# The output projection over two chunks of tokens at a time, with seven block products in place of eight

## The chip, the cores and the metric

The kernel runs on one NeuronCore of one Trainium2 chip. The metric is the device time of one execution in microseconds; 256 and 512 below are columns of a tile, and a tile has up to 128 partitions.

## The reference, cut to what matters

```python
xn = _layernorm(x)                                   # S = 2048 tokens, D = 640
q, k, v = split(xn @ wqkv)                           # H = 32 heads of 20
phi_q = concat(softmax(q @ w_phi), softmax(-(q @ w_phi)))
phi_k = concat(softmax(k @ w_phi), softmax(-(k @ w_phi)))
kv, z = sum_s phi_k * v, sum_s phi_k
o = (phi_q @ kv) / (phi_q @ z + 1e-6)
s = o @ wo                                           # the output projection
g = silu(gelu(xn @ w1 + b1) @ w2 + b2)
return x + s * g
```

The change concerns `s = o @ wo` and what feeds it.

## The kernel before

Everything is computed transposed: features in partitions, tokens in columns. The 2048 tokens are four chunks of 512, worked in the order 2, 3, 0, 1 (`ORDER`). A product in full precision is made of three matmuls (`PASSES`): each operand is split into a high part, rounded by ScalarE (ACT) with a copy, and a low part, what is left, made by a subtraction on VectorE (DVE) or GpSimd (POOL).

The kernel first makes keys, values and queries, then runs twelve units of the gated MLP (six slices of the hidden features, for each half of the tokens), and at last the output projection. From the MLP on, every engine's order is that of the code (`manual_schedule`): each engine works its queue in the order written, and an instruction waits for semaphores of the instructions that it depends on. SP issues all the DMAs of this stretch, so a DMA that waits for its data holds all DMAs behind it.

The attention's numerators belong to the projection's stretch. The normalised query features of a chunk lie in DRAM (`phi_t`); `load_phi` brings them in six tiles `phT`, `num` multiplies each by the state (`bdk`, `bdl`) into a bank of PSUM, ACT copies the high part (`oT[:, 0]`), DVE subtracts to get the low part (`oT[:, 1]`). Five tiles j of 128 rows and a last one of 120 (`oTl`, which holds the remaining 40 rows in three forms) make one chunk. `finish(c, d, oT, last)` is one output tile: chunk c, column block d of five, 16 matmuls into one bank (three for each of five row blocks of `wo`, one for the last rows), a multiplication by the gate on DVE, an addition of the residual on POOL, and the output's DMA. The second half of the tokens (chunks 2 and 3, worked first) reads its gates from DRAM (`gt`); for chunks 0 and 1 ACT makes them in place (`y`). `load_res` loads residual and gate four outputs ahead. Features for a later chunk are loaded in the middle of the chunk before the one that precedes it, and the numerators of the next chunk are computed after its fourth output. The last token tile's features are normalised (`late_q`, `q_norm`) while the first chunk is projected: POOL multiplies, DVE reduces and inverts, POOL scales, DVE transposes, and SP writes them to DRAM.

The pools: `slabs` and `late` hold tiles of 128 x 1024, `rows` is a ring of eleven tiles of up to 704 columns (residuals, gates, raw weights), and eight banks of PSUM rotate (`bankB`). A tile that takes a slot waits for whatever still uses that slot, an output's DMA for instance.

## Time and profile before

| what | value |
|---|---|
| runs, us | 650.24, 650.43, 650.50 (median 650.43) |
| profiled execution, span from first to last instruction | 649.0 us, so that 1.4 us of the median lie around it |
| mean granted TensorE clock | 0.999 |
| TensorE (PE) busy | 643.7 us, 99% |
| DVE, ACT, POOL busy | 485.1 (75%), 238.1 (37%), 408.9 (63%) us |
| DMA, mean over the span | 210 GB/s |
| the last matmuls of the MLP end, the projection's begin | at about 555 us |

A busy share is an average over the span; the stages differ. In the rows below a line such as L1156 is the line of the kernel that recorded the instruction, "pB<-oT,wo" names what is written and read, and PEld is TensorE's loading of weights, which overlaps its matmuls. The matrix products of the numerators are in plain float32 and stand as two records for each instruction. SPq is the queue of SP, from which the DMAs are issued.

### The profile page before, as it was taken

Reading aid. Unit: us, or ns where it says so; the run is one execution under the profiler, and the core shown is the slowest. Engines: PE = TensorE matmul, PEld = TensorE weight load, DVE = VectorE, ACT = ScalarE, POOL = GpSimd, SP = SyncE. Lnnn points to the kernel's source line nnn. Section 1 sums busy time; section 2 is a strip of 40 time slices with the busy share of each in tenths; the row PEclk is TensorE's granted clock in tenths of the full one; section 3 lists DMA queues with packets and bytes.
Section 4 is the critical chain, followed back from the end, with each engine's and each line's share of the span. In section 5 each row is a group of like instructions: output and inputs, shape, how many; then the busy total and the mean of one; then the engine's idle time right before and its main releaser. Section 6 shows DMA issues by size and latency. Waiting matters only on the chain.

```text
span 649.0 us, 11412 instructions
## 1 busy us (share of the span) xinstructions
PE 643.7 (99%) x4379; PEld 559.1 (86%) x4379; DVE 485.1 (75%) x736; ACT 238.1 (37%) x345; POOL 408.9 (63%) x375
## 2 busy tenths in 40 slices
PE   9999999999999999999999999999999999999997
PEld 9999999999999998888888888888888886766866
DVE  5887976789867787587988877768889899853132
ACT  3622423425243447244243346641231524032130
POOL 2876477897987756857878865355463966342321
PEclk9999999999999999999999999999999999999999
DMA  9477286494312477365986998794969499999952
GB/s 346 113 238 228 57 303 197 107 309 147 123 42 74 152 263 262 103 217 170 317 236 236 254 409 285 144 350 163 183 238 243 67 267 198 304 242 248 291 207 81
DMA packets 167119, 136.53 MB, mean 210 GB/s; under 512 B 89890, under 2 KB 131106, under 8 KB 166682
## 3 DMA queue, kind: packets, MB, share of 16 engines
q1 hardware_dynamic: 164330, 124.22, 65.9%
q10 hardware_dynamic: 2736, 11.60, 4.8%
q8 instruction: 34, 0.56, 0.4%
q14 instruction: 19, 0.16, 0.1%
HBM read 87.41 MB, written 48.38 MB: 209 GB/s over the span
## 4 chain that ended last, share of the span: by engine, by line
PE 96%; DMA 1%; DVE 1%; SPq 0%; issue 0%; DVEq 0%
PE pB L998 24%; PE pA L411 23%; PE pB L969 23%; PE pB L1156 11%; PE pA L724 6%; PE pB L1103 2%; PE pA L174 2%; PE kv L491 2%; PE qV L724 1%; DMA folds<-in_wqk_dram 1%; PE qY L724 1%; DVE y L1007 1%; PE pB L1110 1%; DMA phi_t<-eq 0%; PE pA L397 0%; DVE wolh L1080 0%
## 5 line engine op out<-in xcount | busy, mean ns | idle before, releaser
L998 PE MATMUL pB<-hs,w2s 128*128 128x512 f32 x720 | 165.7, 389 | 0.0
L998 PEld LDWEIGHTS pB<-hs,w2s 128*128 128x128 f32 x720 | 135.0, 188 | 28.8 <-DVE y L1007 0.8
L969 PE MATMUL pB<-xp,w1s 128*128 128x512 f32 x324 | 81.3, 389 | 0.0
L969 PE MATMUL pB<-xd,w1s 128*128 128x512 f32 x324 | 79.3, 389 | 0.0
L452 POOL TENSOR_TENSOR eq<-eq,rc 128x1280 f32<-128x1280 f32 x16 | 37.9, 2368 | 55.3 <-DVE rc L1060 38.1
L1156 PE MATMUL pB<-oT,wo 128*128 128x512 f32 (+1 forms) x315 | 72.3, 381 | 0.0
L969 PEld LDWEIGHTS pB<-xd,w1s 128*128 128x128 f32 x324 | 60.8, 188 | 12.6
L969 PEld LDWEIGHTS pB<-xp,w1s 128*128 128x128 f32 x324 | 60.8, 188 | 12.6
L1156 PEld LDWEIGHTS pB<-oT,wo 128*128 128x128 f32 x315 | 57.2, 188 | 13.8 <-PE pB L1103 2.5
L1007 DVE TENSOR_TENSOR y<-pB,y 128x512 f32<-128x512 f32 x100 | 63.1, 676 | 1.4 <-PE pB L998 1.4
L974 ACT ACTIVATE pB<-pB,b1t 128x512 f32<-128x512 f32 x48 | 31.8, 662 | 78.8 <-DVE pB L1237 28.9
L411 PE MATMUL pA<-wk,xp 128*128 128x320 f32 x384 | 59.6, 310 | 0.0
L439 ACT ACTIVATE e<-e 128x1280 f32<-128x1280 f32 x32 | 40.6, 1272 | 50.0 <-POOL e L430 50.0
L411 PEld LDWEIGHTS pA<-wk,xp 128*128 128x128 f32 x384 | 56.9, 188 | 0.1
L430 POOL TENSOR_TENSOR e<-nr,e 128x640 f32<-128x640 f32 x32 | 46.0, 1437 | 16.4 <-DVE nr L429 16.3
L452 POOL TENSOR_TENSOR e<-e,rc 128x1280 f32<-128x1280 f32 x16 | 37.8, 2369 | 20.2 <-DVE rc L479 20.2
L1047 POOL TENSOR_TENSOR ez<-eq,zrep 128x1280 f32<-128x1280 f32 x16 | 47.3, 2959 | 2.0 <-DMA eq<-e_dram 2.0
L519 POOL TENSOR_TENSOR w1s<-raw,w1s 128x640 fp32r<-128x640 f32 (+1 forms) x18 | 26.2, 1458 | 27.6 <-ACT w1s L518 27.6
L411 PE MATMUL pA<-wv,xp 128*128 128x320 f32 x240 | 37.0, 310 | 0.0
L1159 POOL TENSOR_TENSOR xres<-gt,xres 128x256 f32<-128x256 f32 x20 | 14.3, 735 | 35.3 <-DVE gt L1158 24.9
L149 POOL TENSOR_TENSOR w2s<-raw,w2s 128x640 fp32r<-128x640 f32 x23 | 36.1, 1592 | 0.2 <-ACT w2s L147 0.2
L411 PEld LDWEIGHTS pA<-wv,xp 128*128 128x128 f32 x240 | 35.5, 188 | 0.1
(190 smaller groups left out, 1140.4 us busy)
## 6 DMA issues: line engine op xcount, KB each, us to landing
raw<-in_w_dram SPq DMA_DIRECT2D x42, 320.0 KB, 6.7
e_dram<-e ACTq DMA_DIRECT2D x16, 640.0 KB, 3.9
eq<-e_dram SPq DMA_DIRECT2D x16, 640.0 KB
phi_t<-eq SPq DMA_DIRECT2D x64, 160.0 KB, 4.3
phT<-phi_t SPq DMA_DIRECT2D x20, 480.0 KB, 10.1
xt<-in_x_dram SPq DMA_DIRECT2D x16, 320.0 KB, 6.1
xres<-in_xt_dram SPq DMA_DIRECT2D x20, 256.0 KB, 9.1
out_dram<-xres SPq DMA_DIRECT2D x18, 256.0 KB, 5.1
```

The lines of the kernel that those rows point to most:

```text
L149: eng.tensor_tensor(sl[:, 1, :], raw, sl[:, 0, :].bitcast(F32), op=OP.subtract)
L411: nc.tensor.matmul(ps[:, hf, :HALF], stat_x(q, o, k, a), ws[k][:, b, hf * HALF:(hf + 1) * HALF], start=n == 0, stop=n == 3 * KC - 1)
L430: rest = lambda: nc.gpsimd.tensor_tensor(e5[:, :, :, 1, :], nr[:, :, :, None].to_broadcast([P, 2, 16, DH]), e5[:, :, :, 0, :], op=OP.subtract)
L439: nc.scalar.activation(ef, ef, AF.Exp)
L452: nc.gpsimd.tensor_tensor(e3, e3, rc[:, :, None].to_broadcast([P, 64, DH]), op=OP.mult)
L724: nc.tensor.matmul(bank[ch], q_x(blk, a, q), p_weight(base, f, w, k)[:, b], start=ch not in seen and n == 0, stop=n == len(mms) - 1, skip_ ...
L969: nc.tensor.matmul(bank[ch][:], tl[:, a, off + wo_:off + wo_ + P], mov(blk, b), start=new and n == 0, stop=n == len(mms) - 1, skip_group_c ...
L974: nc.scalar.activation(ps, ps, AF.Gelu_apprx_tanh, bias=b1t[:, f:f + 1])
L998: nc.tensor.matmul(ps[:], ws[i][:, b, d * P:(d + 1) * P], hs[o][i][:, a, :], start=i == n == 0, stop=(i, n) == (GF - 1, 2), skip_group_che ...
L1007: nc.vector.tensor_tensor(y, ps[:], y, op=OP.add)
L1047: nc.gpsimd.tensor_tensor(zv, ef, zf, op=OP.mult)
L1156: nc.tensor.matmul(ps[:, mv], w, o[:, mv], start=n == 0, stop=n == 15, skip_group_check=True)
```

## The change

Two chunks, a and b, are projected together: (2, 3), then (0, 1). Four of the five row blocks of `wo` and four of its five column blocks form a 2 x 2 block matrix A (rows 0, 1 against rows 2, 3; columns 0, 1 against 2, 3), and the first four numerator tiles of the two chunks form B: B11 and B21 are a's tiles (0, 1) and (2, 3), B12 and B22 are b's. Strassen's scheme in Winograd's form then needs seven block products:

- of the weights, made once by POOL in `wo_sums`: S1 = A21 + A22, S2 = S1 - A11, S3 = A11 - A21, S4 = A12 - S2;
- of the numerators, made by DVE in PSUM in `num_odd`: T1 = B12 - B11, T3 = B22 - B12, T2 = T3 + B11, T4 = B21 - T2. Each form is split into high and low parts like a plain numerator, by ACT and DVE;
- the products: A11 B11 and A12 B21 give chunk a's columns 0 and 1 (`first_part`); in `second_part`, for column d of 0 and 1, z = S1 T1, v = S3 T3, y = S2 T2, and w = A22 T4, and then S4 B22 is added to z. DVE combines them with the kept A11 B11 (`x1`) into (b, d), (b, d + 2) and (a, d + 2).

The fifth row block and the last rows are multiplied plainly into each output (`tail`); the fifth column block is computed for a in `first_part` and for b in `last_part`, which uses T1 and a kept sum `xt4`. An output's residual and gate are now loaded when the output two before it has been issued (`emit`). Outputs come in the order (a,4) (a,0) (a,1) (b,0) (b,2) (a,2) (b,1) (b,3) (a,3) (b,4). The weights are split in forms of 512 columns, the fifth column block apart (`wo_4`), and the pool `late` has 17 tiles for 13.

Core of the diff:

```diff
+    def split_to(sl, raw):
+        nc.scalar.activation(sl[:, 0], raw, AF.Copy)
+        nc.gpsimd.tensor_tensor(sl[:, 1], raw, sl[:, 0].bitcast(F32), op=OP.subtract)
+        return sl
+
+    def wo_sums(a, b):
+        st = slab(F32, "st", (P, 2, 512))
+        pool = lambda d, p, q, op: nc.gpsimd.tensor_tensor(d, p, q, op=op)
+        pool(st[:, 0, :256], a[:, 256:512], b[:, 256:512], OP.add)
+        pool(st[:, 0, 256:], st[:, 0, :256], a[:, :256], OP.subtract)
+        pool(st[:, 1, :256], a[:, :256], a[:, 256:512], OP.subtract)
+        pool(st[:, 1, 256:], b[:, :256], st[:, 0, 256:], OP.subtract)
+        return [split_to(form(late, "wo"), st[:, i]) for i in (0, 1)]
...
+    def num_even(phi, f, raws, homes):
+        for j in (0, 1, 2, 3, 4, 5):
+            po = num_ps(phi, j)
+            o2 = f["a", j] = form(homes[j])
+            if j == 5:
+                olast(po, o2)
+                yield
+                break
+            ohi(po, o2)
+            if j < 4:
+                r = raws[j] = row([P, CW], F32, "ro")
+                nc.scalar.activation(r[:], po[:], AF.Copy)
+            olo(po, o2)
+            yield
...
+    def num_odd(phi, f, raws, homes):
+        homes = iter(homes)
+        ps, r12 = {}, {}
+        dve = lambda d, a, b, op: nc.vector.tensor_tensor(d[:], a[:], b[:], op=op)
+        new = lambda n, k: f.setdefault((n, k), form(next(homes)))
+        K = (0, 1)
+        for k in K:
+            ps[k] = num_ps(phi, k)
+            r12[k] = row([P, CW], F32, "ro")
+            nc.scalar.activation(r12[k][:], ps[k][:], AF.Copy)
+            dve(ps[k], ps[k], raws[k], OP.subtract)
+            yield
+        for k in K:
+            ohi(ps[k], new("T1", k))
+        for k in K:
+            ps[k + 2] = num_ps(phi, k + 2)
+            ohi(ps[k + 2], new("B22", k))
+            olo(ps[k], f["T1", k])
+            yield
+        for k in K:
+            olo(ps[k + 2], f["B22", k])
+        for n, a, b, op in (("T3", None, r12, OP.subtract), ("T2", None, raws, OP.add), ("T4", raws, None, OP.subtract)):
+            for k in K:
+                p = ps[k + 2]
+                dve(p, p if a is None else a[k + 2], p if b is None else b[k], op)
+            for k in K:
+                ohi(ps[k + 2], new(n, k))
+            for k in K:
+                olo(ps[k + 2], f[n, k])
+            yield
...
+    def outputs(pair):
+        a, b = ORDER[2 * pair:2 * pair + 2]
+        return [(a, 4), (a, 0), (a, 1), (b, 0), (b, 2), (a, 2), (b, 1), (b, 3), (a, 3), (b, 4)]
...
-        steps = [(wo_s[j][:, b, d * P:(d + 1) * P], oT[0][j][:, a, :]) for j in range(5) for a, b in PASSES]
-        steps.append((wols[0][:120, d * P:(d + 1) * P], oT[1][:120, 1, :]))
...
+    def emit(c, d, ps, sl=slice(0, 512), whole=True, fast=False):
+        xr, gt = (xres.pop((c, d)), gates.pop((c, d))) if whole else (xres[c, d], gates[c, d])
+        g = gt[:, sl]
+        nc.vector.tensor_tensor(g, ps[:, sl], g, op=OP.mult)
+        (nc.vector if fast else nc.gpsimd).tensor_tensor(xr[:, sl], g, xr[:, sl], op=OP.add)
+        nc.sync.dma_start(out_t[d * P:(d + 1) * P, c * CW + sl.start:c * CW + sl.stop], xr[:, sl])
+        if whole:
+            i = next(done)
+            load_res(i + 2)
+            gate(i + 2)
...
+    def first_part(pair, f, hook):
+        a, b = ORDER[2 * pair:2 * pair + 2]
+        ps = bankB()
+        steps = [m for k in (0, 1) for m in passes(d4(k), f["a", k])]
+        acc(ps, steps, last=False)
+        keep_ = slab(F32, "xk", (P, 2, 512))
+        xt4 = slab(F32, "xk", (P, 2, 512))[:, 0]
+        nc.scalar.activation(xt4, ps[:], AF.Copy)
+        hook()
+        acc(ps, [m for k in (0, 1) for m in passes(d4(k + 2), f["a", k + 2])] + tail(f, "a", 4), False)
+        emit(a, 4, ps)
+        for d in (0, 1):
+            hook()
+            ps = bankB()
+            acc(ps, [m for k in (0, 1) for m in passes(wt("A11", k, d), f["a", k])], last=False)
+            nc.scalar.activation(keep_[:, d], ps[:], AF.Copy)
+            hook()
+            acc(ps, [m for k in (0, 1) for m in passes(wt("A12", k, d), f["a", k + 2])] + tail(f, "a", d, "A1k"), False)
+            emit(a, d, ps)
+        return keep_, xt4
...
+    def second_part(pair, f, d, x1, hook, fast):
+        a, b = ORDER[2 * pair:2 * pair + 2]
+        dve = lambda o, p, q: nc.vector.tensor_tensor(o, p, q, op=OP.add)
+        z, v, y = bankB(), bankB(), bankB()
+        acc(z, two(f, "S1", d, "T1"))
+        hook()
+        acc(v, two(f, "S3", d, "T3"))
+        hook()
+        acc(y, two(f, "S2", d, "T2"))
+        dve(x1, y[:], x1)
+        u3 = row([P, CW], F32, "u3")
+        dve(u3[:], v[:], x1)
+        tz = row([P, CW], F32, "tz")
+        dve(tz[:], z[:], x1)
+        hook()
+        w = bankB()
+        acc(w, two(f, "A22", d, "T4") + tail(f, "a", d + 2, "A2k"))
+        hook()
+        acc(z, two(f, "S4", d, "B22") + tail(f, "b", d, "A1k"), False)
+        dve(z[:], z[:], x1)
+        emit(b, d, z)
+        hook()
+        acc(v, tail(f, "b", d + 2, "A2k"), False)
+        dve(v[:], v[:], tz[:])
+        emit(b, d + 2, v)
+        dve(w[:], w[:], u3[:])
+        emit(a, d + 2, w, fast=fast)
+        hook()
...
+    def last_part(pair, f, xt4, end):
+        a, b = ORDER[2 * pair:2 * pair + 2]
+        xr, gt = xres[b, 4], gates[b, 4]
+        nc.gpsimd.tensor_tensor(xt4, xt4, gt[:, :], op=OP.mult)
+        nc.gpsimd.tensor_tensor(xr[:], xt4, xr[:], op=OP.add)
+        steps = [m for o, q in (("T1", 0), ("B22", 2)) for k in (0, 1) for m in passes(d4(k + q), f[o, k])]
+        steps += tail(f, "b", 4)
+        parts = (slice(0, W2), slice(W2, 512)) if end else (slice(0, 512),)
+        for n, sl in enumerate(parts):
+            ps = bankB()
+            acc(ps, steps, mv=sl)
+            emit(b, 4, ps, sl, n + 1 == len(parts), end)
...
+            wo_f = [wo_sums(wo_r[k], wo_r[k + 2]) for k in (0, 1)]
...
-            load_res(ci * KC + d + 4)
-            finish(c, d, oT, ci == NCH - 1 and d >= 3)
...
-            if ci + 2 < NCH and d == 1:
-                phi = load_phi(ORDER[ci + 2], JA, late if ci % 2 else None)
-            if ci + 1 < NCH and d == 3:
-                num(phin, oTn, range(6))
-            if ci + 2 < NCH and d == 3:
-                phin = {**phi, **load_phi(ORDER[ci + 2], JB)}
...
+    odd = num_odd(phin, f0, raws0, [None] * 8 + [late] * 2 + [None] * 2)
+    x1, xt4 = first_part(0, f0, hooks([(odd, 2)], [(odd, 2)], [(odd, 1)], [(odd, 1)], [(odd, 1)]))
+    for _ in odd:
+        pass
+    phi = load_phi(ORDER[2], (0,))
+    f1, raws1 = {}, {}
+    even = num_even(phi, f1, raws1, [late] * 4 + [None] * 2)
+
+    def more_phi(js):
+        for j in js:
+            phi.update(load_phi(ORDER[2], (j,)))
+            yield
+
+    mp = more_phi((1, 2, 3, 4, 5))
+    second_part(0, f0, 0, x1[:, 0], hooks([(lq, 2)], [(lq, 2), (mp, 1)], [(lq, 2)], [(lq, 1)], [(lq, 1)], [(lq, 4), (mp, 3)]), False)
+    second_part(0, f0, 1, x1[:, 1], hooks([], [(even, 1), (mp, 1)], [(even, 1)], [(even, 1)], [(even, 1)], [(even, 2)]), False)
+    phin = load_phi(ORDER[3], (0, 1, 2, 3))
+    phin.update(load_phi(ORDER[3], (4, 5), late))
+    last_part(0, f0, xt4, False)
+    odd = num_odd(phin, f1, raws1, [None] * 8 + [late] * 2 + [None] * 2)
+    x1, xt4 = first_part(1, f1, hooks([(odd, 2)], [(odd, 2)], [(odd, 1)], [(odd, 1)], [(odd, 1)]))
+    for _ in odd:
+        pass
+    second_part(1, f1, 0, x1[:, 0], hooks(), False)
+    second_part(1, f1, 1, x1[:, 1], hooks(), True)
+    last_part(1, f1, xt4, True)
```

**Where instructions move.** The first place is ACT at the end of the MLP. `wo` are the weights' high parts, `oT` the numerators' high parts. Before:

```order
L976 ACTIVATE hs<-pB 128x512
L147 ACTIVATE wo<-raw 128x640 x5
L1106 ACTIVATE oT<-pB 128x512 x5
L1112 ACTIVATE oTl<-pB 120x512
L1106 ACTIVATE oT<-pB 128x512 x5
```

And now, where `st` are POOL's sums of weights and `ro` a plain copy of a numerator, kept for the forms:

```order
L1126 ACTIVATE wo<-raw 128x512 x5
L1126 ACTIVATE wo_5811<-raw 128x640
L1126 ACTIVATE wo<-st 128x512 x4
L1110 ACTIVATE oT<-pB 128x512
L1150 ACTIVATE ro<-pB 128x512
L1110 ACTIVATE oT<-pB 128x512
L1150 ACTIVATE ro<-pB 128x512
```

Four copies that wait for POOL's sums now stand between the weights and the first numerator, and each of the first four numerators is copied twice.

The second place is SP's queue where the features of the third and the fourth chunk are loaded (`phi_t_82` is chunk 0, `phi_t_83` chunk 1, to which the last token tile is also written). Before, around the third chunk's loads:

```order
L1163 DMA out_dram<-xres 128x512
L1091 DMA phT<-phi_t_82 120x2x512 x3
L1130 DMA xres<-in_xt_dram 128x512
L1134 DMA gt<-g_dram 128x512
L1163 DMA out_dram<-xres 128x512
L1130 DMA xres<-in_xt_dram 128x512
L1134 DMA gt<-g_dram 128x512
L1163 DMA out_dram<-xres 128x512
L1091 DMA phT<-phi_t_82 120x2x512 x2
L1093 DMA phT<-phi_t_82 80x512
```

Now, from the last token tile's writes on:

```order
L1069 DMA phi_t_83<-eq 32x40x32 x4
L1250 DMA out_dram<-xres 128x512
L1206 DMA xres<-in_xt_dram 128x512
L1210 DMA gt<-g_dram 128x512
L1250 DMA out_dram<-xres 128x512
L1206 DMA xres<-in_xt_dram 128x512
L1210 DMA gt<-g_dram 128x512
L1250 DMA out_dram<-xres 128x512
L1206 DMA xres<-in_xt_dram 128x512
L1210 DMA gt<-g_dram 128x512
L1091 DMA phT<-phi_t_82 120x2x512 x3
L1093 DMA phT<-phi_t_82 80x512
```

Three outputs, the tile's writes, and the loads that follow each output stand ahead of four of the six feature loads. The loads of chunk 1 stand likewise behind the three outputs (b,1), (b,3) and (a,3).

The third place is TensorE in the first part, column 0 of the second pair, with the semaphores that it waits for. Before, an output is one run of matmuls:

```order
L1156 MATMUL pB<-oT,wo 128x512 [waits PE_49]
L1156 MATMUL pB<-oT,wo 128x512 x14
L1156 MATMUL pB<-oTl,wol 128x512
L1156 MATMUL pB<-oT,wo 128x512 [waits PE_49]
L1156 MATMUL pB<-oT,wo 128x512 x14
L1156 MATMUL pB<-oTl,wol 128x512
```

Now there is a wait for ACT after six matmuls, since ACT has to copy the first half sum before the second is added to it:

```order
L1240 MATMUL pB<-oT,wo 128x512 [waits PE_49]
L1240 MATMUL pB<-oT,wo 128x512 x5
L1240 MATMUL pB<-oT,wo 128x512 [waits Activation_49]
L1240 MATMUL pB<-oT,wo 128x512 x8
L1240 MATMUL pB<-oT,wol 128x512
```

That copy stands in ACT's queue between copies of forms, which wait for DVE.

## The prediction, made before the changed kernel was run

> **What bounds the kernel now.** I read the page's busy shares first, then the stretch of the output projection, then the chain that ended last, then the groups of the operations that the change adds, and last the queue of SP.

> ```profile
> span 649.0 us, 11412 instructions
> PE 643.7 (99%) x4379; PEld 559.1 (86%) x4379; DVE 485.1 (75%) x736; ACT 238.1 (37%) x345; POOL 408.9 (63%) x375
> ...
> core 0: us, PE busy (x) PEld busy (x) DVE busy (x) ACT busy (x) POOL busy (x), PEclk, DMA share, GB/s
> 555.40:645.20 89.80, 89.70 (x408) 65.41 (x406) 37.86 (x74) 18.27 (x29) 30.88 (x38) 1.00 0.83 235
> ...
> 569.93 4.44 PE pB L1103 x20
> 575.24 18.47 PE pB L1156 x80
> 593.71 4.44 PE pB L1103 x20
> ```

> TensorE has work for 99% of the span, and the table by stretches says the same of the projection alone: 89.70 of 89.80 us, at full clock, while DVE works 37.86. So every matmul removed is worth its whole time, and every wait of TensorE in this stretch, of which there is none now, costs its whole length. The chain's pieces show the price: 18.47 us for five outputs of 16 matmuls, 0.231 us each, and 4.44 us for ten numerator matmuls (20 records), 0.444 each. The question is whether the other queues can serve TensorE through the longer dependency of the new order.

> **1. Matmuls removed.** A pair of chunks has ten outputs of 16 matmuls, 160. The new code issues 16 + 32 in the first part, 42 for each of two column indices in the second, 16 in the last: 148. Two pairs save 24 matmuls: 24 x 0.231 = **-5.5**. The numerators stay at 12 per chunk.

> **2. Start of the projection.** ACT and POOL make the weight forms ahead of the first numerators' copies.

> ```profile
> 539.04 7.68 POOL L149 TENSOR_TENSOR wo<-raw,wo 128x640 fp32r<-128x640 f32 x5 [3.03 <-ACT wo L147]
> 547.55 0.60 ACT L1106 ACTIVATE oT<-pB 128x512 fp32r<-128x512 f32 x1 [6.08 <-PE pB L1103]
> 555.18 3.56 PE L1156 MATMUL pB<-oT,wo 128*128 128x512 f32 x15
> ...
> L519 POOL TENSOR_TENSOR w1s<-st,w1s 128x512 fp32r<-128x512 f32 x18 | 23.0, 1298 | 0.0
> L507 POOL TENSOR_TENSOR st<-raw 128x256 f32<-128x256 f32 x18 | 13.3, 740 | 9.0 <-PE pB L969 5.2 <-DMA w_dram<-w1s 3.7
> L1106 ACT ACTIVATE oT<-pB 128x512 fp32r<-128x512 f32 x20 | 12.0, 598 | 60.9 <-PE pB L1103 42.7 <-DMA phi_t<-eq 17.9 <-DMA out_dram<-xres 0.3
> L1107 DVE TENSOR_TENSOR oT<-pB,oT 128x512 fp32r<-128x512 f32 x20 | 13.0, 683 | 2.1 <-ACT oT L1106 1.9
> 525.29 1.28 DVE L1007 TENSOR_TENSOR y<-pB,y 128x512 f32<-128x512 f32 x2
> ```

> The first two rows say that numerators are copied by ACT at 547.55 while POOL ends its splits at 546.7; the third that the projection begins at 555.18. The groups below price what is added: a 512-wide low part on POOL 1.30 us, a 256-wide sum 0.74, an ACT copy 0.60, a DVE operation on 512 columns 0.68, or 0.64 from one to the next as in the last row. Now POOL starts at the same 539.0: five low parts 6.5 and one of 640 columns 1.57, to 547.1; four sums 3.0, to 550.1; two low parts 2.6, to 552.7; four sums, to 555.7. ACT's last form copy needs the last sum, and ACT is in order, so only at 556.3 does it copy the first numerator (0.6), then its plain copy (0.6), then DVE's low part (0.64): 558.2, with 0.3 of hand-overs 558.5. TensorE stands 558.5 - 555.2 = **+3.3**. What POOL does after (to 561) meets nothing due. The extra DMA, 0.3 MB of weights, lands before 547 and is put at nothing, covered by POOL's first five splits.

> **3. First part, both pairs.** TensorE may go on in a bank only after ACT has copied its first half sum. For column 4 ACT has eleven copies from 556.3, 6.6 us, to 563.1 with 0.2 of hand-over; TensorE is there after six matmuls and four numerators, 558.5 + 1.4 + 1.8 = 561.7: 1.4. For column 0 nothing stands between the halves: one copy and hand-over, 0.9. For column 1 the copy stands in ACT behind T2's copies, which wait for DVE's sums; one form is two sums, a copy, two low parts, 1.28 + 0.6 + 1.28 + 0.2 = 3.4, with the gate multiplication 4.0, against 3.7 for TensorE's 16 matmuls, and DVE starts behind: 0.9 + 1.3 = 2.2. Together 4.5; in the second pair the first of them lies under item 6, 3.0. **+7.5**, between 3.6 (two bare copies with hand-over a pair) and 10 (a lag of 1.3 more in each pair).

> **4. Second part, first column.** The bank of the product Z may be written again only after DVE has read it. From 558.5 TensorE has 76 matmuls (17.6), 12 numerators (5.3) and the waits of 4.5: 585.9. DVE must by then do 33 operations of 0.64 (21.1), wait some 3 us for ACT, and serve the last token tile.

> ```profile
> L447 DVE TENSOR_REDUCE dn<-ez 128x64 f32<-128x1280 f32 x2 | 2.9, 1446 | 0.0
> L1050 DVE RECIPROCAL rc<-rc 128x64 f32<-128x64 f32 x1 | 0.6, 554 | 0.0
> L1064 DVE STREAM_TRANSPOSE eq<-eq 128x1280 f32<-128x1280 f32 x4 | 5.9, 1496 | 1.1 <-POOL eq L452 1.1
> L452 POOL TENSOR_TENSOR eq<-eq,rc 128x1280 f32<-128x1280 f32 x2 | 4.7, 2361 | 1.1 <-DVE rc L1060 1.1
> ```

> The rows price a transpose, two reductions and a reciprocal at 1.50 + 2 x 1.45 + 0.55 = 5.0: 558.5 + 21.1 + 3 + 5.0 = 587.6, with hand-overs 588.2. **+2.3**, bounded by 0 (ACT's waits overlap the tile's work) and 6.

> **5. Features of the third chunk.** SP now issues them far ahead; in the change their loads stand behind an output that is itself late.

> ```profile
> 574.15 1.58 SPq L1091 DMA_DIRECT2D phT<-phi_t  x3
> 582.38 2.69 SPq L1091 DMA_DIRECT2D phT<-phi_t  x2
> SPq L1163 <- POOL xres L1159: 17.8, 6, 7.3
> ...
> phT<-phi_t SPq DMA_DIRECT2D x20, 480.0 KB, 10.1
> DMA to landing us min/median/max: 5.1/10.1/10.9
> xres<-in_xt_dram SPq DMA_DIRECT2D x20, 256.0 KB, 9.1
> DMA to landing us min/median/max: 2.3/5.6/9.1
> ```

> The first two rows stand 11 to 20 us ahead of the numerators at 593.71; the third is SP waiting for POOL before an output, its whole queue behind it; the last four are size and landing time of a feature load and of a residual. From 588.2 DVE ends the tile's denominators (1.5), POOL scales it (2.4), DVE transposes it (1.5), and only then, in order, come Z's sum and gate multiplication (1.4): 595.0. POOL adds (1.3); SP issues that output and the residual and gate of the output two further on, three issues of 0.36: 597.4. They land after 2.3 at least; behind the tile's own feature writes I take 3.5: 600.9. DVE multiplies by that gate (0.64), POOL adds (1.3), SP issues three more and comes to the features: 604.0, with hand-overs 604.3. A feature load lands after 3.3 (2.3, and 224 KB more at the stretch's 235 GB/s) to 5.1; I take the middle, 4.2: 608.5. TensorE has from 588.2 only 42 matmuls and four numerators, 9.7 + 1.8: 599.7. **+8.8**, between 5.5 and 11.

> **6. Features of the last chunk.** From 608.5 TensorE has 36 matmuls and eight numerators, 8.3 + 3.6: 620.4. The loads stand in SP behind the output (a, 3). ACT's plain copy of a numerator waits for a row slot whose output must first land (617.3); its 0.6, DVE's low part, two sums and two multiplications bring 621.2, POOL 622.5, SP's issues 623.5, the load 627.7: 7.3. The next loads come 2.1 apart (480 KB at 235 GB/s) for 0.9 of numerators each: 1.3 more. **+8.6**, between 5 and 12.

> **7. The end.** M is the end of the last matmul.

> ```profile
> 644.82 0.28 PE L1156 MATMUL pB<-oTl,wol 120*128 120x256 f32 x1
> 645.60 0.42 DVE L1159 TENSOR_TENSOR xres<-y,xres 128x256 f32<-128x256 f32 x1
> ```

> Now DVE ends at M + 0.9. In the change (b, 1) leaves TensorE at M - 4.8 (the last 32 half matmuls and four more); DVE 1.4, POOL 1.3 and SP 1.0 with hand-overs bring the load of (a, 3)'s residual to M - 1.1, its landing to M + 1.2; that of (b, 4) is 1.4 behind, POOL adds to it (1.3), and DVE has three operations of 0.42 left: M + 5.2. **+4.3**, between 1 and 6.

> **8. Clock.** TensorE is left idle for longer than anywhere before.

> ```profile
> 411.39 0.44 PE pB L923 x4
> 0.84 4.18 PE L555 MATMUL pA<-const-float32-1.0 128*128 128x128 f32 x18 [0.84 <-PEq L1402]
> 646.00:647.00 1.00, 0.00 (x0) 0.00 (x0) 0.02 (x1) 0.00 (x0) 0.00 (x0) 1.00 0.09 32
> 648.00:649.00 1.00, 0.00 (x0) 0.00 (x0) 0.00 (x0) 0.00 (x0) 0.00 (x0) 0.50 0.00 0
> ```

> The clock is whole a us after the last matmul and half three us after it. At the kernel's start 18 matmuls of 128 columns take 4.18, at 411 four take 0.44: 4.18 - 18 x 0.11 = 2.2 lost before full rate. I count it once, behind item 5; behind item 6 the half rate lies beside loads 2.1 apart. **+2.2**, between 0 and 6.6 (three waits). [...]

> Sum: -5.5 + 3.3 + 7.5 + 2.3 + 8.8 + 8.6 + 4.3 + 2.2 = +31.5. The profiled span of 649.0 becomes 680.5; the runs' median, 650.43, lies 1.4 above that span, which I leave: 681.9, **682 us**.

> **Rivals.** *Everything is hidden, and only item 1 is left:* 650.4 - 5.5 = 645, at the best. For it: DVE has 52 of 90 us free and gets 52 operations more (a pair 14 for the forms, 12 to combine products), 33 us. It decides where items 2 to 8 stay under 5.5 together; the form work on POOL alone is 3.3 by measured durations, and the features of both later chunks would have to be asked for 9 us sooner. 0.03, and 0.02 for a near balance. *The loads are in time, the engines' chains not:* if (b, 0)'s sum comes early, DVE's gate wait vanishes and items 5, 6 and 8 go: 682 - 8.8 - 8.6 - 2.2 = 662. For it: the SP queue has little else to do then. Against it: it is in order, and the tile's transposes stand ahead. 0.12. *Worse:* every hand-over 0.1 longer on some 60 links, feature loads at 5.1, and three clock losses: 682 + 6 + 2 + 4.4 = 694 and above. 0.11. That the matmuls aren't saved is excluded by the count of the new order. My forecast, all terms near their values: 0.72.

> The range: all lower bounds at once would give 663, all upper ones 700. That they fall together is unlikely; some two thirds of the way to each, 668 to 694, leaves no more than 2 in 10 outside. A change under 0.2%, 1.3 us, could not be told from none. Faster 0.03, same 0.02, slower 0.95.

> **What would show it.** Matmuls of the projection 24 fewer; TensorE's share down from 99% to about 94% (638 of 680); first projection matmul near 558.5; two waits of TensorE for feature loads of 7 to 9 us, near 600 and 620 on this axis; short ones for ACT in the first parts; DVE waiting for a gate load; a clock line that falls after a long wait; the last DVE operation some 5 us behind TensorE. Wrong it would be if SP's loads proved early enough, or if DVE's waits for ACT overlapped its queue more than I let them.

## The result, and the profile after

| | median, us | runs |
|---|---|---|
| before | 650.46 | 650.24 to 651.11 |
| changed | 693.16 | 691.78 to 695.16 |

The ratio is 1.0658, interval 1.0638 to 1.0678: 42.7 us slower, 11 more than the 31.5 forecast. The profiled execution took 691.78 us with a span of 689.8 (before: 649.0); it is the fastest of the four, 1.4 below the median. The page of the changed kernel has these rows; the last one is the granted clock in 40 slices of 17.2 us:

```profile
span 689.8 us, 11461 instructions
PE 648.6 (94%) x4355; PEld 555.1 (80%) x4355; DVE 516.3 (75%) x768; ACT 256.1 (37%) x380; POOL 422.4 (61%) x374
...
PEclk9999999999999999999999999999999999977897
```

TensorE has 24 matmuls fewer and is busy 4.9 us longer; the clock row falls in the slices of the projection. DVE's share of the span is the 75% it was, and from the first projection matmul to the last it works 69.0 of 122.6 us, so that its amount of work does not fill the stretch. What TensorE waited for from 540 on (engine, line, what ended the wait, us in all, times, longest):

```profile
PE pB L1102 <- DMA phT<-phi_t: 21.1, 2, 11.2
PE pB L1240 <- ACT xk L1274: 4.9, 4, 1.8
PE pB L1240 <- DVE oT L1113: 3.5, 1, 3.5
PE pB L1240 <- DVE tz L1282: 1.5, 1, 1.5
PE pB L1240 <- ACT xk L1266: 0.2, 1, 0.2
```

Before, it waited 0.39 us from 540 on, now 31.2. L1102 are the numerators, L1240 the block products; xk is the tile that keeps the half sums. The order of events, from the timeline: first the weight forms and the first projection matmul, then the chain to the third chunk's features, then the end.

```profile
554.38 0.63 ACT L1126 ACTIVATE wo<-st 128x512 fp32r<-128x512 f32 x1 [3.36 <-POOL st L1132]
558.13 0.73 PE L1240 MATMUL pB<-oT,wo 128*128 128x512 f32 x2 [3.50 <-DVE oT L1113]
...
590.29 1.51 DVE L1064 STREAM_TRANSPOSE eq<-eq 128x1280 f32<-128x1280 f32 x1 [2.54 <-POOL eq L452]
591.73 0.67 DVE L1282 TENSOR_TENSOR pB<-pB,xk 128x512 f32<-128x512 f32 x1
598.75 0.39 PE L1240 MATMUL pB<-oT,wol 120*128 120x512 f32 x1
600.64 0.69 DVE L1248 TENSOR_TENSOR gt<-pB,gt 128x512 f32<-128x512 f32 x1 [5.58 <-DMA gt<-g_dram]
604.16 1.36 SPq L1091 DMA_DIRECT2D phT<-phi_t  x3
610.37 1.97 PE L1102 MATMUL pB<-phT,bdk 120*64 120x512 f32 x4 [11.23 <-DMA phT<-phi_t]
...
680.44 0.28 PE L1240 MATMUL pB<-oT,wol 120*128 120x256 f32 x1
684.19 1.26 POOL L1313 TENSOR_TENSOR xres<-xk,xres 128x512 f32<-128x512 f32 x1 [2.66 <-DMA xres<-in_xt_dram]
686.28 0.42 DVE L1249 TENSOR_TENSOR xres<-y,xres 128x256 f32<-128x256 f32 x1
```

The middle rows are the chain of item 5: the token tile's transpose waits for POOL, the sum of (b, 0) stands behind it, TensorE has run out of work at 599.1, DVE stands 5.58 us at a gate that was asked for only when the output two before had gone, SP comes to the features at 604.16, and TensorE gets them at 610.37. The last rows are item 7: POOL's addition for the last column waits 2.66 us for a residual, and DVE ends at 686.70, 6.0 behind TensorE's last matmul (before: 0.9).

### The profile page after: what moved, and what is told of

Its sections match the earlier page's. It is cut to its first block, busy times and chain, and to the rows that moved or that the text cites. A ratio compares the mean times of both kernels' runs of the same rounds, so it can differ in the third digit from the quotient of the medians.

```text
span 689.8 us, 11461 instructions
## 1 busy us (share of the span) xinstructions
PE 648.6 (94%) x4355; PEld 555.1 (80%) x4355; DVE 516.3 (75%) x768; ACT 256.1 (37%) x380; POOL 422.4 (61%) x374
## 5 line engine op out<-in xcount | busy, mean ns | idle before, releaser
L1240 PE MATMUL pB<-oT,wo 128*128 128x512 f32 (+1 forms) x291 | 72.4, 397 | 10.1 <-ACT xk L1274 4.9
L969 PE MATMUL pB<-xp,w1s 128*128 128x512 f32 x324 | 81.3, 390 | 0.0
L1240 PEld LDWEIGHTS pB<-oT,wo 128*128 128x128 f32 x291 | 52.8, 193 | 33.5 <-ACT xk L1274 6.6
L969 PE MATMUL pB<-xd,w1s 128*128 128x512 f32 x324 | 79.3, 390 | 0.0
L452 POOL TENSOR_TENSOR eq<-eq,rc 128x1280 f32<-128x1280 f32 x16 | 37.9, 2369 | 60.2 <-DVE rc L1060 43.0
L969 PEld LDWEIGHTS pB<-xd,w1s 128*128 128x128 f32 x324 | 60.8, 188 | 12.6
L969 PEld LDWEIGHTS pB<-xp,w1s 128*128 128x128 f32 x324 | 60.8, 188 | 12.5
L1007 DVE TENSOR_TENSOR y<-pB,y 128x512 f32<-128x512 f32 x100 | 63.1, 676 | 1.4 <-PE pB L998 1.4
L452 POOL TENSOR_TENSOR e<-e,rc 128x1280 f32<-128x1280 f32 x16 | 37.8, 2368 | 20.1 <-DVE rc L479 20.1
L519 POOL TENSOR_TENSOR w1s<-raw,w1s 128x640 fp32r<-128x640 f32 (+1 forms) x18 | 26.2, 1458 | 28.5 <-ACT w1s L518 28.5
L1102 PE MATMUL pB<-phT,bdk 120*64 120x512 f32 x80 | 22.7, 678 | 21.2 <-DMA phT<-phi_t 21.1
L1249 POOL TENSOR_TENSOR xres<-gt,xres 128x512 f32<-128x512 f32 x10 | 12.8, 1278 | 43.5 <-DVE gt L1248 38.8
L1113 DVE TENSOR_TENSOR oT<-pB,oT 128x512 fp32r<-128x512 f32 x32 | 21.0, 686 | 23.1 <-ACT ro L1150 20.4
## 6 DMA issues: line engine op xcount, KB each, us to landing
xres<-in_xt_dram SPq DMA_DIRECT2D x20, 256.0 KB
out_dram<-xres SPq DMA_DIRECT2D x19, 256.0 KB
```

The source lines that it names most:

```text
L452: nc.gpsimd.tensor_tensor(e3, e3, rc[:, :, None].to_broadcast([P, 64, DH]), op=OP.mult)
L519: nc.gpsimd.tensor_tensor(sl[:, 1, :n], src, sl[:, 0, :n].bitcast(F32), op=OP.subtract)
L969: nc.tensor.matmul(bank[ch][:], tl[:, a, off + wo_:off + wo_ + P], mov(blk, b), start=new and n == 0, stop=n == len(mms) - 1, skip_group_c ...
L1007: nc.vector.tensor_tensor(y, ps[:], y, op=OP.add)
L1102: nc.tensor.matmul(po[64 * e:64 * e + 64, :], bdk[:120, 2 * j + e, :], ph[:120, e, :], start=True, stop=True)
L1240: nc.tensor.matmul(ps[:, mv], w, o[:, mv], start=first and n == 0, stop=last and n == len(steps) - 1, skip_group_check=True)
```

## The experiments

Each experiment is the changed kernel with an edit, of which the core is shown; combined_tile7 stands on combined, w_first on combined_tile7 and numerators_grouped on w_first, and the last one, spread_before, edits the kernel before. Times are medians of runs in one series with the kernel before, which stands at 650.29 to 650.78 in them. The changed kernel was not run again beside them: it stands at 693.16, between 691.78 and 695.16, and a gain of 2 us is at the edge of what such a comparison can tell.

**The loads: early_loads**

```diff
-    phi = load_phi(ORDER[2], (0,))
+    phi = load_phi(ORDER[2], (0, 1, 2, 3), late)     # right behind the first part
...
-    even = num_even(phi, f1, raws1, [late] * 4 + [None] * 2)
+    even = num_even(phi, f1, raws1, [None] * 6)      # forms go to slabs
+    # last chunk: load_phi(ORDER[3], (j,), late) behind each (even, 1)
```

> The features of the third chunk are asked for as soon as the first part of pair 1 is issued, four of them into the slots of `late` that the first four numerator tiles give back, and the features of the last chunk one after another, each behind the numerators of the third chunk that free its slot; all work of the engines stays. My theory (the two long waits, 11.2 and 9.9 us, are the place of the loads in SP's queue and their slots, and 3.5 to 4 us of the half clock follow from them): both waits shrink to a few us, TensorE never stops for 10 us, and the time falls by 12 to 20 us, to 673 to 681. The waits that remain in pair 1 are DVE's: up to 4 us at the second bank Z. Rival (DVE's 52 added operations bound this stretch, the loads are only what is seen last): the waits for features go, waits of the same length for DVE appear in their place, and the time falls by less than 4 us, to 689 or more. Rival (the long waits go, but the clock loss has another cause): the waits fall by some 18 us, and the clock line still shows 0.5 after 600.

Measured: 681.78 us, 11.4 less, ratio 1.0492 (1.0476 to 1.0508), just short of the 12 to 20. TensorE's waits:

```profile
PE pB L1240 <- ACT xk L1274: 6.7, 4, 2.4
PE pB L1240 <- DVE tz L1282: 6.6, 2, 5.1
PE pB L1240 <- DVE oT L1113: 3.5, 1, 3.5
PE pB L1240 <- ACT xk L1266: 2.3, 1, 2.3
PE pB L1102 <- DVE oT L1113: 1.5, 1, 1.5
```

The 21.1 us for features are gone, and 10.6 of the 31.2 in all; a wait of 5.1 for DVE has come up at the second bank Z. That looks like the rival in which DVE is the bound. DVE's own timeline says what it is:

```profile
603.14 0.69 DVE L1248 TENSOR_TENSOR gt<-pB,gt 128x512 f32<-128x512 f32 x1 [6.84 <-DMA gt<-g_dram]
606.47 0.80 PE L1240 MATMUL pB<-oT,wo 128*128 128x512 f32 x1 [5.08 <-DVE tz L1282]
```

DVE stood idle for 6.84 us at the same gate load, with the sums for Z queued behind it. So it is SP's order again, by its other load: the gate is asked for at 598.70, behind the token tile's writes and an output, and DVE goes on 4.4 us later. Item 5 was two waits one behind the other, and taking out the second alone uncovers the first.

**SP's order alone: outputs_pool_queue**

```diff
-        nc.sync.dma_start(out_t[...], xr[:, sl])
+        nc.gpsimd.dma_start(out_t[...], xr[:, sl])
```

> One word: the outputs' DMAs are issued from POOL's queue, behind the addition that makes them, and no longer from SP's. Nothing else moves; the loads keep their places and slots. My theory of item 5 (the loads stand in SP behind outputs that wait for POOL, up to 12.2 us): SP's waits for POOL vanish, the residual, gate and feature loads go out as soon as their slots are free, and the two long waits fall from 11.2 and 9.9 us to about 5 and 8; what is left of them is slots that are not yet free. Time 3 to 7 us less, 686 to 690. Rival (slots alone, not the order in SP): the waits stay at 10 or more and the time within 1.5 us of 693. Rival (POOL, which must now issue DMAs as well, is late itself): slower than 693.

Measured: 689.33 us, 3.8 less, ratio 1.0597 (1.0581 to 1.0614). First TensorE's wait for features, then two of SP's (changed kernel first, this one second):

```profile
PE pB L1102 <- DMA phT<-phi_t: 16.5, 2, 9.2
...
SPq L1250 <- POOL xres L1249: 81.0, 16, 12.2
...
SPq L1206 <- DMA out_dram<-xres: 25.1, 4, 9.1
```

In the changed kernel SP waits 81.0 us for POOL in front of outputs. With the outputs elsewhere it waits for row slots that an output's landing gives back (25.1), and the long waits are 7.3 and 9.2 for 11.2 and 9.9. So the order in SP is worth about 4 us, as expected in size, but the long waits stayed longer than the 5 and 8 us that I expected: a part of what I had put down to the order belongs to the slots.

**The start: late_forms**

```diff
-        return [split_to(form(late, "wo"), st[:, i]) for i in (0, 1)]   # in wo_sums
+        return st
...
+    ws = wo_split()      # yields after each of the four split_to
+    x1, xt4 = first_part(0, f0, hooks([(odd, 2), (ws, 1)], [(odd, 2), (ws, 1)], ...))
```

> The four splits of the weight forms S1 to S4 are issued one by one in the first part, behind steps of the second chunk's numerators, and no longer ahead of the first chunk's numerators; POOL's sums stay where they were. My theory (item 2: ACT waits for POOL's sums ahead of the first copies): the 3.5 us wait at the first projection matmul falls to under 0.5, and all behind moves up, to about 690. Rival (the stretch behind is set by DMA landings, so what is won at the start is waited for later): the first wait goes and the wait for the third chunk's features grows by the same 3 us, 693 unchanged. The added copies may lengthen ACT's waits in the first part by up to 1 us in all.

Measured: 687.62 us, 5.5 less, ratio 1.0580 (1.0562 to 1.0598). The first projection matmul comes at 553.92, 4.2 earlier, with no wait:

```profile
553.92 1.52 PE L1240 MATMUL pB<-oT,wo 128*128 128x512 f32 x6
PE pB L1102 <- DMA phT<-phi_t: 20.6, 2, 11.6
```

The waits for features keep their length (20.6 for 21.1), so the gain isn't waited for later: the chain to the features moves with the start. TensorE's last matmul ends 4.5 earlier. The time fell by more than the wait of 3.5 and the 690 expected; the 2 us beyond are within the spread of the runs of these kernels (1.5 to 3.4 us) and not explained.

**The half sums: halves_apart**

```diff
+        # order of the first part: half col 4 | half col 0 | rest col 4 | half col 1 | rest col 0 | rest col 1
+        q0 = half(0)     # A11 product, ACT copies it
+        acc(ps, ... d4(k + 2) ... + tail(f, "a", 4), False); emit(a, 4, ps)
+        q1 = half(1)
+        rest(0, q0); rest(1, q1)
```

> In the first part the half sums are issued ahead: half of column 4, half of column 0, rest of column 4, half of column 1, rest of 0, rest of 1, so that ACT has 9 to 16 matmuls to copy a half sum where it had none or four. All operations stay. My theory (item 3: TensorE waits for the copy): the four waits of 0.7 to 1.8 us behind ACT go, 4.9 us in all. In pair 1 the outputs come a little earlier or later but the feature loads of the third chunk stand behind the second part's outputs, so what is won there may be waited for at the feature loads or at the bank Z; pair 2 has nothing behind it that could take the gain. So 690 to 691 with the gain of pair 2 alone (2.5), 688 with both. Rival (DVE, not ACT, is late in the first part): the waits move to DVE's sums at the start of the second part, and the time stays within 1 us of 693.

Measured: 687.20 us, 6.0 less, ratio 1.0562 (1.0547 to 1.0576).

```profile
PE pB L1102 <- DMA phT<-phi_t: 19.7, 2, 9.9
PE pB L1240 <- DVE tz L1293: 3.7, 1, 3.7
```

All ACT waits of the first part are gone (5.1); 2.2 of them come back at bank Z (3.7 for 1.5), and the feature waits are 1.4 shorter. TensorE's idle time falls by 4.3 us, its end comes 4.4 earlier, and the runs show 6.0; the difference of 1.6 is as large as the 1.7 at which I put one clock step (an estimate, below), and no larger than the spread of the runs.

**The clock: filled_clock**

```diff
+        for n in range(fill):      # 40 ahead of the third chunk's numerators, 34 ahead of the last's
+            nc.tensor.matmul(po[:], wo_s[0][:, 0, :P], f0["T1", 0][:, 0, :], start=True, stop=True)
```

> Only matmuls without use are added: 40 of 512 columns ahead of the first numerators of the third chunk, 34 ahead of those of the last, each into the bank that the numerators overwrite, on operands that lie ready; at 0.227 us they take 9.1 and 7.7 us of waits of 11.2 and 9.9. If the half clock costs what the changed kernel's trace seems to show (half rate for 4.1 and 3.4 us behind the two long waits and 3.4 us near 652, some 5.4 us lost), the clock line stays at 1 and the time falls by 4 to 5.5 us, to 688 to 689, while the waits together with the filling keep their 21 us. My forecast had 2.2 for this. If the wait for the features hides it (TensorE at half rate only while the next loads are awaited anyway), the time changes by less than 1.5 us. If the filling delays the numerators, it rises.

Measured: 691.30 us, 1.9 less, ratio 1.0627 (1.0610 to 1.0644). The interval overlaps that of the changed kernel (1.0638 to 1.0678): not the 4 to 5.5 expected, and hardly to be told from nothing. In the changed kernel's trace the granted clock falls to 0.50 at 604.29, 628.18 and 652.08 and is back at 1.00 at 614.53, 638.42 and 655.49: from one change to the next 3, 4, 3, 4 and 1 times 3.41 us. The rows below cut the span into steps of that length (stretch, its length, TensorE's busy time and instructions, clock, DMA share, GB/s). First the changed kernel, then filled_clock, then early_loads:

```profile
553.09:556.50 3.41, 1.55 (x7) 1.00 1.07 256
556.50:559.92 3.42, 1.79 (x8) 1.00 1.01 331
...
648.66:652.08 3.42, 1.64 (x8) 1.00 0.32 110
652.08:655.49 3.41, 3.41 (x10) 0.50 0.12 44
...
633.03:636.45 3.42, 1.68 (x7) 1.00 1.02 259
636.45:639.86 3.41, 2.34 (x5) 0.50 1.00 243
639.86:643.27 3.41, 3.41 (x9) 0.50 0.96 262
...
555.13:558.55 3.42, 0.54 (x2) 1.00 1.05 308
558.55:561.96 3.41, 3.41 (x9) 0.50 1.00 360
619.99:623.40 3.41, 1.87 (x8) 1.00 0.60 166
623.40:626.81 3.41, 1.11 (x6) 1.00 0.24 90
626.81:630.23 3.42, 3.42 (x10) 0.50 0.85 268
```

In these rows the clock went to 0.50 behind steps in which TensorE was busy for 0.54, 1.11, 1.64 and 1.68 us of 3.41; behind 1.55, 1.79 and 1.87 it stayed at 1.00, so that from 1.55 to 1.68 both occur. Idle were 1.8 us of the step at 648.66 and 2.3 of that at 623.40. So the filling did remove the long idle stretches, but the 2.5 us that it left, and two of 1.65 and 1.15, were followed by half steps of their own: 3.41 us at 612.55 and 6.82 from 636.45; a third lies behind the start's wait, at 558. In this profile TensorE worked 12.6 us at half rate, against 10.9 in the changed kernel's, so this run does not price the clock. (The profiled execution, 692.71 us, is the slowest of its four.)

The wait of 1.8 us ahead of 651.17 was followed by a step of 3.41 us at half rate, which I put at 1.7 us, half of it, an estimate. The same wait of 3.5 us at 558 was followed by none in the changed kernel, where it is spread over two steps (TensorE busy for 1.55 and 1.79), and by one in early_loads (0.54). If the place on the steps decides, that would also give the spread of the changed kernel's runs, 3.4 us where the kernel before has 0.9. The mean clock of every run is on record: 0.978 in the fastest and 0.971 in the slowest, where one half step takes 0.0025 off the mean; but the two runs between (692.33 at 0.973, 693.99 at 0.974) do not follow that order, and the steps are recorded only in profiled executions, so this isn't shown.

**Forms, half sums and loads together: combined**

```diff
+            z2 = bankB(); acc(z2, two(f, "S4", d, "B22") + tail(f, "b", d, "A1k"))
+            dve(z2[:], z2[:], tz[:]); emit(b, d, z2)       # for: acc(z, ...), dve(z, z, x1)
...
+    EARLY = {1: (3, 4), 2: (5, 6), 13: (15, 16), 14: (17, 18), 15: (19,)}   # load_res in emit, ahead of the output
...
+            if not end:
+                nc.vector.tensor_tensor(ps[:], ps[:], xt4, op=OP.add)       # last_part; POOL's two go
```

> All findings together on the changed kernel: forms split in the first part (late_forms), half sums ahead (halves_apart), features of later chunks early (early_loads), and six things more: the product S4 B22 goes to a bank of its own and DVE adds it to the kept sum tz, so no bank waits for DVE; DVE's work for the last token tile stands behind the products' sums; residuals and gates of four outputs of pair 1 and five of pair 2 are loaded earlier, ahead of the output's DMA in SP; one plain copy of a numerator lies in the unused half of xt4's tile and takes no row; in pair 1 DVE adds xt4 and POOL's two operations for it go; in pair 2 these two come ahead of the last column. Operation counts on DVE stay within one of the changed kernel's. My theory (nearly all of the 43 us are hand-overs and loads, none of it DVE's amount of work): TensorE's waits fall from 31 us to 4 to 10, its last matmul comes at 646 to 653 on the trace's axis, DVE ends under 2 us behind it, 650 to 658 us. Rival (DVE is the bound with 52 more operations): waits for DVE of 10 us or more stay, 665 or above.

Measured: 656.64 us, 36.5 less than the changed kernel, ratio 1.0100 (1.0087 to 1.0114). TensorE's last matmul ends at 649.59, DVE 1.9 behind it.

```profile
PE pB L1102 <- DMA phT<-phi_t: 2.4, 2, 1.2
PE pB L1102 <- DVE oT L1113: 2.0, 1, 2.0
```

Of 31.2 us of waits 4.4 are left, 2.0 of them for DVE, with as many operations on DVE. That settles the rival of DVE's added operations: the page counts 769 of them here and 768 in the changed kernel, so DVE's amount of work was not the bound. The run does not say what each of the edits gave.

**The last token tile out of the way: combined_tile7**

```diff
-    QN = {1: (8,), 2: (9,), 3: (10,), 4: (11,), 5: (12, 13), 7: (14, 15), 8: (0, 1), 9: (2, 3), 10: (4, 5), 11: (6,)}
+    QN = {1: (8,), 2: (9,), 3: (10,), 4: (11, 12), 5: (13, 14), 7: (15, 0), 8: (1, 2), 9: (3, 4), 10: (5, 6), 11: (7,)}
```

> As the run combined, and the last token tile is normalised in the MLP: the schedule of tiles over the units becomes one tile fuller in unit 4 and shifts by one, so that nothing of a tile's normalisation but the last transposes and writes stands in the projection. DVE loses there 5 us of reductions, denominators and transposes in pair 1, POOL 5.3 us, and two tiles of `slabs` come free. If DVE and slots are what is left to wait for in pair 1 (my theory), TensorE's waits fall to 1 to 5 us and the time to 643 to 650, with the MLP unchanged. Rival: the MLP, in which TensorE had no idle time, waits for DVE or POOL in unit 4 by as much as the tile's work, 5 us, and the sum is no better than the run combined.

Measured: 651.00 us, ratio 1.0008 (0.9996 to 1.0019): as fast as before, within what can be told, and 1 us outside the 643 to 650 expected. Waits for features are gone, and the MLP did not pay: its last matmul ends at 554.6, as in the changed kernel. The longest of TensorE's waits:

```profile
PE pB L1242 <- DVE oT L1113: 0.8, 1, 0.8
```

TensorE now waits 1.0 us in all in this stretch, at full clock, and yet ends only 1.7 us earlier than before (643.42 for 645.10), where 24 matmuls fewer should give 5.5. Of the 3.8 that are missing only the 1.0 is waits.

**The order at the end, and groups of numerators: w_first, numerators_grouped**

```diff
+        dve(w[:], w[:], u3[:]); emit(a, d + 2, w)     # w_first: ahead of z2, no longer last
...
-    hooks([], [(even, 1), ...], [(even, 1), ...], [(even, 1), ...], [(even, 1), ...], [(even, 2)])
+    hooks([], [], [(even, 3), ...], [], [(even, 3), ...], [])       # numerators_grouped
```

> As combined_tile7, but in the second part the sum w + u3 and its output (a, d + 2) come ahead of the product S4 B22 and its two outputs, and the last of these outputs adds its residual on POOL. At the end of the kernel DVE then has four operations between the last full bank and the last half banks, not seven. In combined_tile7's profile TensorE ends at 643.42 (before: 645.10) and DVE at 645.37, 1.95 behind it (before: 0.92). Expected: DVE ends about 0.9 behind TensorE, and the 0.83 us wait near 609 goes: 1.5 to 2 us less, 649.0 to 649.5. Rival (the last DMAs set the end, whatever DVE does): unchanged, 651.

> As w_first, and the six numerators of the third chunk are computed three and three and no longer in five places. In combined_tile7's trace a matmul at which TensorE goes over to the numerators, or comes back from them, takes 0.32 or 0.34 us from its start to the next one's, where the others take 0.227, and the numerators between them about 0.05 to 0.1 more: some 0.3 us for each group of numerators. The changed kernel has eight groups more than the kernel before, 2.4 us of the 5.5 that the saved matmuls give. Three groups fewer: 0.9 us less than w_first, 648.0 to 648.6, and below 650.5. Rival (the longer matmuls belong to the bank changes, not to the numerators): no difference to w_first.

Measured: w_first 649.34 us, ratio 0.9983 (0.9974 to 0.9991), 1.7 less than combined_tile7; numerators_grouped 649.66, ratio 0.9985 (0.9977 to 0.9994), no faster than w_first and not the 648.0 to 648.6 expected. In w_first DVE ends 0.9 behind TensorE's last matmul, as forecast:

```profile
642.92 0.28 PE L1242 MATMUL pB<-oT,wol 120*128 120x256 f32 x1
643.69 0.43 DVE L1255 TENSOR_TENSOR xres<-y,xres 128x256 f32<-128x256 f32 x1
```

For the groups, the projection's stretch as a whole, w_first and then numerators_grouped (columns: PE, PEld, DVE, ACT, POOL busy with instructions, then clock, DMA share, GB/s):

```profile
554.56:643.20 88.64, 87.93 (x385) 59.67 (x383) 63.34 (x98) 34.55 (x61) 33.13 (x26) 1.00 0.75 224
...
554.62:643.93 89.31, 87.21 (x385) 59.91 (x383) 63.28 (x98) 34.38 (x61) 33.09 (x26) 1.00 0.76 218
```

With the same 385 instructions TensorE is busy 0.72 us less for three groups fewer, as a price by the group would have it; but its idle time grew from 0.7 to 2.1, for features again, and the time stayed.

**The price of a group by itself: spread_before**

```diff
 # the kernel before
+                    if n % 3 == 2:
+                        between()          # one numerator tile behind every third matmul of the fourth output
-                num(phin, oTn, range(6))
+                num(phin, oTn, (5,))
```

> The kernel before, with the six numerators of the next chunk no longer in one place behind the fourth output, but one behind every third matmul of that output and the last behind the output. No operation is added, nothing waits there before (TensorE's waits in the whole stretch are 0.39 us), and three chunks make 15 groups of numerators more. If a group costs TensorE some 0.24 to 0.3 us by itself (0.72 us for three in numerators_grouped against w_first; 0.3 by the longer matmuls at its ends), the time rises by 3.6 to 4.5 us, to 654 to 655. Rival (the longer matmuls are those of new banks or of waits that the records do not name, not of the change to plain float32 and back): unchanged, 650.5, or up by less than 1.

Measured: 655.75 us, 5.0 above the 650.78 of its series, ratio 1.0077 (1.0063 to 1.0092). Before, then this kernel, over the projection, and all that TensorE waited for in it:

```profile
555.18:645.10 89.92, 89.92 (x409) 65.60 (x407) 38.02 (x73) 18.27 (x29) 30.88 (x38) 1.00 0.83 235
...
555.25:649.87 94.62, 94.62 (x406) 62.73 (x404) 37.35 (x72) 18.16 (x29) 30.97 (x38) 1.00 0.77 218
PE pB L1110 <- DVE y L1007: 0.4, 1, 0.4
```

No wait was added, and TensorE is busy 4.7 us longer for 15 groups more. A group cost 0.31 to 0.33 us here, a little more than expected, and the rival that nothing is added falls. A change of bank alone is not the reason: in the trace of the kernel before, TensorE goes from the last matmul of an output to the first of the next one, in another bank, in 0.232 us from start to start, against 0.227 within a bank, but over to a numerator in 0.32, and the first matmul behind the numerators takes 0.34. The numerators differ from the other matmuls both in type (plain float32) and in shape (120x64 weights for 128x128); which of the two is paid for isn't shown. The change has eight groups more than before (eleven for three behind the first chunk's), 2.6 us: half of what its 24 matmuls save.

## Why the forecast held in kind and fell short in size

| item | forecast, us | in the trace | by experiment |
|---|---|---|---|
| 1 matmuls | -5.5 | 24 fewer | net -2.9 with the groups |
| 2 start | +3.3 | 3.5 waited, first matmul at 558.13 (forecast 558.5) | 5.5 (late_forms) |
| 3 half sums | +7.5 | 5.1 | 6.0 (halves_apart) |
| 4 bank Z | +2.3 | 1.5 | 3.7 without the ACT waits ahead of it |
| 5 third chunk's features | +8.8 | 11.2 | with 6: 11.4 (early_loads) |
| 6 last chunk's features | +8.6 | 9.9 | see 5 |
| 7 end | +4.3 | 5.1 | w_first has it gone |
| 8 clock | +2.2 | 5.5 (estimate) | not priced (filled_clock) |
| groups of numerators | not in the sum | | 2.6 (spread_before: 0.33 each) |

- **Item 2** held: the chain of ACT behind POOL's sums came out at 558.13.
- **Items 3 and 4** were of the right kind and 3.2 too high together. Most of it is column 4 of the first pair: 1.4 us forecast, 0.2 in the trace, while column 1 has 1.7 and 1.8 for 2.2. I took ACT's eleven copies at 0.6 us each, which is about what one lasts; the rows below are the first of them and start 0.47 and 0.48 apart, as do the others, so that TensorE could go on at 561.81, not 563.1. ACT's queue had to be priced from start to start. Items 3 and 4 also share one cover, so that what one loses the other partly takes.

```profile
556.29 0.58 ACT L1110 ACTIVATE oT<-pB 128x512 fp32r<-128x512 f32 x1
556.76 0.59 ACT L1150 ACTIVATE ro<-pB 128x512 f32<-128x512 f32 x1
557.24 0.60 ACT L1110 ACTIVATE oT<-pB 128x512 fp32r<-128x512 f32 x1
```

- **Item 5's chain** is in the trace as forecast, link by link: TensorE out of work at 599.1 (599.7), SP at the features at 604.16 (604.3). The step that was too small is the load: I took 4.2 us, the middle of 3.3 and 5.1, and it was 5.8 from the end of the issue at about 604.5 to the matmul at 610.37, behind a residual and a gate only. Both bounds were too low. I had priced one load by itself; between issue and use, 604.16 to 610.37, the DMA engines were 85% busy and moved 245 GB/s, 1.5 MB, as much as three such loads, and two more stood right behind it. That these slowed the first is likely, but no run issues one alone.
- **Item 6's chain** is there too, some 4 us later than forecast and 7 at its end: ACT's copy waits for an output's landing until 621.35 (617.3), SP comes to the features at 627.76 (623.5), and TensorE, out of work at 625.1 (620.4), goes on at 635.05 (627.7). Again the load was too small, 7.3 from issue to use for 4.2. The 1.3 for the loads behind it did not occur. Items 5 and 6 together measured 21.1 for 17.4.
- **Item 8** is the term most mis-sized: 5.5 for 2.2, an estimate, half of TensorE's time at half rate behind the waits (4.2 behind the first, 3.4 behind the second, 3.4 at 652; from 652.32 to 654.46 its matmuls start 0.427 us apart, at 1.00 they start 0.227 apart). I counted one loss; there were three, as my upper bound had it. The second I had taken to lie beside the loads behind item 6; the row below (stretch, length, TensorE's busy time, clock, DMA share, GB/s) shows TensorE at work for nearly all of that step, so the loads did not hide it. The third follows a wait of 1.8 us, in item 3, for which I had no clock term.

```profile
635.00:638.40 3.40, 3.29 (x8) 0.50 1.03 249
```

- **Not seen at all**: the price of groups of numerators, 2.6. Item 1 took each operation at its duration in the old order; the change also multiplied the places at which TensorE goes over to the numerators. TensorE's share came out at the 94% forecast, but by luck: it was busy 648.6 of 689.8 us, not 638 of 680, because half rate and groups are busy time too.
- The terms as measured (the clock's 5.5 as estimated above) give -5.5 + 31.2 - 0.4 + 5.5 + 2.6 = 33.4 for TensorE's last matmul, and 35.6 were measured (645.10 to 680.72); with 5.2 more from there to the span's end that is 40.8 on the span. Of the 2.2 that are left some 1.5 lie beside the waits for ACT and DVE: across such a wait the time from one matmul's start to the next is 0.16 us more than the wait and the usual 0.227, and the first matmul behind the wait takes 0.11 more (six waits, of which five lie between two matmuls of the projection). So such a wait cost TensorE some 0.27 more than its length, where the forecast took just that. The last 0.7 aren't explained.
- **Luck.** The time lies at the upper edge of the range, 668 to 694. The 3.2 us by which items 3 and 4 were too high made up for part of what items 5 to 8 and the groups lacked; with these two at their size the forecast would have been 679.
- **The rivals**: that everything is hidden fell at every item. "The loads in time, the engines' chains not" (662) did not occur, and early_loads, which made the features early, came to 682 and not 662, because the gate's load stood in the same queue. The worst case (694 and above, chance 0.11) lies nearer to the measured time than my 682 does: it had the three clock losses, and feature loads at 5.1, which was still too little. For the first rival I counted 52 more operations on DVE; the page has 32 more (768 for 736), mainly because the gate multiplications are no longer made in halves, 21 in place of 40. The busy time rose by 31.2 us, close to the 33 that I gave.

## What to carry to other kernels

A scheme that saves products pays with longer dependencies: before its arithmetic is priced, follow each queue that is issued in order (loads behind outputs, sums behind an unrelated tile) to where TensorE runs out of work; here the waits were 31 us, and, as combined shows, DVE's added operations gave none of them by their amount. When waits lie one behind the other, taking out the last one uncovers the one before, so take them out together: single edits gave 2 to 11 us; forms, half sums and loads together, with the further moves of combined, the token tile's and w_first's, gave 44, to 649.34 us for 650.49 before. And count how often TensorE changes the kind of matmul, not only how many matmuls there are.
